# Top-k attention and a hard-swish feed-forward on one core: blocks of 128 tokens at an even rate, later reciprocals, and transposes of Keys and queries by DMA

## The chip, the cores and the metric

The kernel runs on one core of a Trainium2 chip. The core has five engines that work through their own queues of instructions in order and wait for each other by semaphores: TensorE (PE in the profile, with its weight loads as PEld) for matrix products, VectorE (DVE), ScalarE (ACT), GpSimd (POOL), and SyncE (SP), which here issues all DMAs. The metric is the device time of one execution in microseconds (us), lower is better; the median of several executions is compared.

## The reference

```python
q, k, v: (8, 8, 576, 64) float32            # batches, heads, tokens, head size
scores = (1 / sqrt(64)) * q @ k.T           # per batch and head: 576 x 576
kth = 32nd largest of each row
scores = where(scores >= kth, scores, -1e9)
attn = exp(scores - max); attn = attn / (sum(attn) + 1e-9)
x = (attn @ v) with the heads side by side  # 4608 tokens x 512
h = x @ w_in                                # 512 -> 2048
g = h * clip(h + 3, 0, 6) / 6
out = g @ w_out                             # 2048 -> 512
```

The two weight matrices arrive as float64 and are turned into float32 in the kernel.

## The kernel before, in words

**Units of work.** A *pair* is two heads of a batch (four pairs per batch, 32 in all). A *duo* is 128 queries of two pairs, which makes four rows of 576 scores on each partition, two per pair; the two pairs are the halves of the duo, u = 0 and 1. As 576 is 4 x 128 + 64, each batch has eight normal duos and two *rest* duos for the last 64 queries of both heads; a rest duo has half as many rows. Eight batches give 80 duos. In batches 0 to 2 the rest duos are at the end of the batch, in batches 3 to 6 they stand at places 2 and 7 of its ten duos (counted from 0), in batch 7 at places 2 and 3.

**One duo, in steps.** `scores` (L200 on): TensorE multiplies queries with Keys into the one large PSUM tile `big` (L215 to L230), ScalarE copies them to SBUF as `sc` (L219, L220, L233, L236; three buffers). `top` (L250, L254): VectorE finds the 32 largest of each row in four rounds of MAX8 and MATCH_REPLACE8. `shift` (L263, L266): GpSimd computes the bias of the exponential. `exp` (L273, L278, L283): ScalarE makes masked exponentials and their sums `den`. `inverse` (L287): VectorE takes the reciprocal of `den`. `weights` (L297, L306): GpSimd scales the rows and splits each float32 into two 16-bit halves, `e16`. `flip` (L312): SyncE issues a DMA transpose of those halves into `t16`. `join` (L318): ScalarE (u = 0) or GpSimd (u = 1) puts the halves together again as `eT`, now transposed. `values` (L338, L345): TensorE multiplies with the values into a PSUM tile `pv`, and ScalarE copies that at once to `xT` (for rest duos `xr`), the input of the feed-forward.

**Feed-forward.** A block is 128 or 256 tokens. The first product (L362) makes 512 columns of `h` at a time; ScalarE makes relu(h + 3) and a copy (L370, L372), GpSimd caps and multiplies (L376, L377); the second product (L384) sums up 16 parts for 128 tokens, ScalarE scales by 1/6 (L394) and SyncE stores. The generator `feed_forward` hands the work out in *pieces*: 16 for 128 tokens, 32 for 256. A piece of the first product is 16 TensorE instructions at 128 tokens and 8 of double width at 256; a piece of the second is 4. Each float32 product counts as two matmul instructions in the profile. The gates on GpSimd are issued two pieces behind their product.

**Order.** The order of all work is written out by hand: 80 x 8 slots and a few more at the end. In slot i of duo m VectorE's round i of the duo comes first, then the steps of this and earlier duos that are due by a table (`usual`, `early` for the first two duos, `soon` for the last two: the numbers are slots counted from the start of the duo), then some pieces. The scores of duo m + 1 are issued in slot 1 of duo m. How many pieces a duo gets is set at its start from `left`, the pieces that are queued: 6, 7, 8 or 9 for a normal duo, 3, 4, 4 or 5 for a rest duo, at less than 8, from 8, from 16 and from 48. A block takes 256 tokens where enough pieces are queued when its first half ends (L480, `state["half"]`). Ahead of value products, pieces are issued without a break until the buffer of `xT` that is to be written is free (`while ... piece()`).

**Keys and queries.** For each pair `load` (L146 on) brings Keys and queries to SBUF. `transpose` (L171 on) turns them on TensorE, nine transposes (L177) into `big`, and ScalarE copies to `kq` and `kr` (L179, L180, L183). The pairs of the next batch are loaded in slot 0 of duos 4 to 7 of a batch and transposed in slot 5 of duos 5 to 8.

Of the kernel before, what the change touches and what calls it, by code (L numbers as in the profile page):

```python
# [10 lines left out]
F32 = mybir.dt.float32  # L11
# [18 lines left out]
def kernel(  # L30
# [22 lines left out]
    def pool(name, bufs, **kw):  # L53
        return ctx.enter_context(tc.tile_pool(name=name, bufs=bufs, **kw))

    consts = pool("consts", 1)
    kqpool = pool("kq", 13)
    scpool = pool("sc", 3)
    wkpool = pool("wk", 1)
    mpool = pool("m", 4)  # L60
    xtpool = pool("xt", 2)
    xrpool = pool("xr", 1)
    gpool = pool("g", 8)
    hpool = pool("h", 2)
# [74 lines left out]
    class Pair:  # L139
# [31 lines left out]
        def transpose(self):  # L171
            kq = kqpool.tile([P, JP + S], F32, tag="kq", name="kq")
            self.kT, self.qT = kq[:, 0:JP], kq[:, JP : JP + S]
            ps = big()
            for j in range(2 * J + 1):
                rows = self.landed[:, j, :, :].rearrange("p h d -> p (h d)")
                nc.tensor.transpose(ps[:, j * P : (j + 1) * P], rows, ident[:])  # L177
            c0 = 2 * JP
            nc.scalar.copy(kq[:, 0:c0], ps[:, 0:c0])  # L179
            nc.scalar.copy(kq[:, c0 : c0 + R], ps[:, c0 + R : c0 + 2 * R])  # L180
            for hh in range(2):
                d = slice(hh * D, (hh + 1) * D)
                nc.scalar.copy(self.kr[d, hh, :], ps[d, c0 : c0 + R])  # L183

    class Duo:

# [139 lines left out]
        def values(self, dst):  # L326

            w = R if self.rest else P
            pv = ps_w.tile([P, 512], F32, tag="w", name="pv")
            for u in range(2):  # L330
                pr, eT = self.pairs[u], self.eT[u]
                for c in range(J + 1):
                    for hh in range(2):
                        if self.rest:
                            rhs = eT[:, c if c < J else J + hh, hh * R : (hh + 1) * R]
                        else:
                            rhs = eT[:, c if hh == 0 or c == J else J + 1 + c, :]
                        nc.tensor.matmul(  # L338
                            pv[hh * D : (hh + 1) * D, u * w : (u + 1) * w],
                            pr.vm[:, hh, c, :] if c < J else pr.vr[:, hh, :],  # L340
                            rhs,
                            start=(c == 0),
                            stop=(c == J),
                        )
            nc.scalar.copy(dst, pv[:, 0 : 2 * w].rearrange("p (u q) -> p u q", u=2))  # L345

    def feed_forward(xT, nt, rows):

        gs = []
        nf = 512 // nt
        for f0 in range(0, NFC, nf):
            h = ps_w.tile([P, 512], F32, tag="w", name="h")
            for f in range(f0, f0 + nf):
                if f == f0 + nf // 2:
                    yield None  # L360
                for i in range(NHP):
                    nc.tensor.matmul(  # L362
                        h[:, (f - f0) * nt : (f - f0 + 1) * nt],
                        w_in[:, i, f * P : (f + 1) * P],
                        xT[:, i, 0:nt],
                        start=(i == 0),
                        stop=(i == NHP - 1),
                    )
            g = gpool.tile([P, 512], F32, tag="g", name="g")
            nc.scalar.activation(g[:], h[:], AF.Relu, bias=three[:], scale=1.0)  # L370
            hs = hpool.tile([P, 512], F32, tag="h", name="hs")
            nc.scalar.copy(hs[:], h[:])  # L372
            gs.append(g)

            def gate(g=g, hs=hs):
                nc.gpsimd.tensor_scalar(g[:], g[:], 6.0, 0.0, ALU.min, ALU.max)  # L376
                nc.gpsimd.tensor_tensor(g[:], g[:], hs[:], ALU.mult)  # L377

            yield gate
        for t0 in range(0, nt, P):  # L380
            acc = ps_w.tile([P, DM], F32, tag="w", name="acc")
            for f in range(NFC):
                c0 = f % nf * nt + t0
                nc.tensor.matmul(  # L384
                    acc[:],
                    gs[f // nf][:, c0 : c0 + P],
                    w_out[:, f, :],
                    start=(f == 0),
                    stop=(f == NFC - 1),
                )  # L390
                if f % 2 == 1:
                    if f == NFC - 1:
                        o = opool.tile([P, DM], F32, tag="o", name="o")
                        nc.scalar.mul(o[:], acc[:], 1.0 / 6.0)  # L394
                        for p0, p1, dst in rows(t0):
                            nc.sync.dma_start(dst, o[p0:p1, :])
                    yield None

# [40 lines left out]
    def queue(*block):  # L441
        nonlocal left
        todo.append(feed_forward(*block))
        if block[0] is not state.get("xr"):
            blocks.append(todo[-1])
        left += block[1] // 8

    state = {}

    def values(m):  # L450

        u = duos[m]
        b, qt, hp = u.pairs[0].b, u.qt, u.pairs[0].hp
        if u.rest:
            if b % 2 == 0 and hp == 0:
                while state.get("rest") in todo:
                    piece()
                state["xr"] = xrpool.tile([P, NHP, P], F32, tag="xr", name="xr")
            u.values(state["xr"][:, hp : hp + 2, (b % 2) * R : (b % 2 + 1) * R])
            if b % 2 == 1 and hp == 2:  # L460

                def rows(t0):
                    return [
                        (i * R, (i + 1) * R, out[(b - 1 + i) * S + JP : (b + i) * S, :])
                        for i in range(2)
                    ]

                queue(state["xr"], P, rows)
                state["rest"] = todo[-1]
            return  # L470

        if hp == 0 and not state.get("half"):
            while len(blocks) > 1 and blocks[-2] in todo:
                piece()
            state["xT"] = xtpool.tile([P, NHP, 2 * P], F32, tag="xT", name="xT")
        c0 = P if state.get("half") else 0
        u.values(state["xT"][:, hp : hp + 2, c0 : c0 + P])
        if hp == 0:
            return
        state["half"] = not c0 and b < B - 1 and qt % 2 == 0 and left >= (24 if b < 3 else 4)  # L480
        if not state["half"]:

            def rows(t0):
                t = qt - c0 // P + t0 // P
                return [(0, P, out[b * S + t : b * S + JP : J, :])]

            queue(state["xT"], c0 + P, rows)

    chunks = list(weight_chunks())
    landing, converting, adding = [], [], []  # L490
# [25 lines left out]
    def pair_at(m, first):  # L516

        b, at = divmod(m, per_batch)
        return pairs[b + 1][at - first] if b + 1 < B and 0 <= at - first < NHP else None
# [16 lines left out]


    usual = dict(
        shift0=3, exp0=4, inverse0=7, weights0=8, flip0=10, join0=13,
        shift1=7, exp1=8, inverse1=11, weights1=12, flip1=14, join1=17, values=20,  # L540
    )
    early = dict(
        shift0=3, exp0=3, inverse0=4, weights0=4, flip0=5, join0=8,
        shift1=7, exp1=7, inverse1=8, weights1=8, flip1=9, join1=12, values=12,
    )
    soon = dict(
        shift0=3, exp0=3, inverse0=5, weights0=5, flip0=7, join0=10,
        shift1=7, exp1=7, inverse1=9, weights1=9, flip1=11, join1=14, values=16,
    )
    queued = {}  # L550
    for m in range(ND):
# [3 lines left out]
    def parts(slot, late=None):  # L555

        for m, part in sorted(queued.get(slot, []), key=lambda x: x[1][:-1] != "shift"):
            if late is not None and (part[:-1] in ("inverse", "weights")) != late:
                continue
            if part == "values":  # L560
                values(m)
            else:
                getattr(duos[m], part[:-1])(int(part[-1]))

    for m in range(ND + 3):
        u = duos[m] if m < ND else None

        level = (left >= 8) + (left >= 16) + (left >= 48)
        count = ((3, 4, 4, 5) if u and u.rest else (6, 7, 8, 9))[level]
        for i in range(8):  # L570
            if u:
                u.top(i // 4, i % 4)
# [14 lines left out]
                for p in duos[i // 4].pairs:  # L587
                    p.load_values()
            if i == 0:
                p = pair_at(m, 4)  # L590
                if p:
                    p.load()
            if i == 3 and u and u.pairs[0].b and 1 <= m % per_batch <= 2:
                for p in duos[m - 1].pairs:
                    p.load_values()
            if i == 5:
                p = pair_at(m, 5)
                if p:
                    p.transpose()
            piece((i + 1) * count // 8 - i * count // 8)  # L600
    while todo:
        piece()
    piece(2)
# [33 lines left out]
```

## Time and profile before

| | before |
|---|---|
| median of 10 executions | 1628.43 us (1627.47 to 1630.53) |
| the profiled execution | 1628.88 us |
| its span, first to last instruction | 1627.1 us |
| TensorE, VectorE busy | 1468.9 us, 1465.8 us |
| GpSimd, ScalarE busy | 1140.1 us, 1094.6 us |
| mean granted clock of TensorE | 0.960 |

In a row of the profile, L312 is line 312 of the kernel; `out<-in` are the program's names of the tiles; xN is a count; `busy, mean` are us in all and ns of one instruction; behind the second bar stands the idle time of the engine just before them, and what ended it. Rows of the chain and of the timeline begin with the start and the length in us; in brackets stands the idle time before and what ended it. Rows of waits read: who (engine, tile, line) waited for whom, us in total, times, longest.

### The profile page before, as it was taken

What the parts mean: (1) busy time and instruction counts of PE and PEld (TensorE: products, weight loads), DVE (VectorE), ACT (ScalarE), POOL (GpSimd) and SP (SyncE); (2) the same over time, 40 slices, a digit from 0 to 9 for tenths busy, and PEclk for the clock granted to TensorE, in tenths of its full rate; (3) what the DMA queues carried; (4) which work ended last, traced back from release to release, by engine and by line L of the source; (5) the groups of instructions that cost most, each with busy time, mean ns of one, the idle gap of its engine ahead of it and who ended that gap; (6) DMA issues with size and microseconds to landing.
All of it is one profiled execution on the core that took longest, in us unless ns stands there. A gap on an engine that the chain in (4) does not pass through costs nothing.

```text
span 1627.1 us, 26916 instructions
## 1 busy us (share of the span) xinstructions
PE 1468.9 (90%) x9376; PEld 999.9 (61%) x9376; DVE 1465.8 (90%) x3105; ACT 1094.6 (67%) x1865; POOL 1140.1 (70%) x1264
## 2 busy tenths in 40 slices
PE   5254989889999999988989999899999999899999
PEld 2152657566666776666657575647567584657875
DVE  6999999999999978999999999999999989999500
ACT  6675876767776577667768676767777676757521
POOL 4778676777867776766678596767687776867741
PEclk9577999999999999999999999999999999999999
DMA  8552543445334442445344533444454424433310
GB/s 229 149 181 59 95 99 71 84 98 95 73 87 90 87 88 52 102 88 109 71 86 87 114 66 80 99 101 83 75 101 93 94 56 92 83 62 71 65 22 13
DMA packets 450312, 144.37 MB, mean 89 GB/s; under 512 B 433280, under 2 KB 441472, under 8 KB 450176
## 3 DMA queue, kind: packets, MB, share of 16 engines
q1 hardware_dynamic: 450176, 142.65, 42.5%
q8 instruction: 74, 1.21, 0.3%
q14 instruction: 62, 0.51, 0.1%
HBM read 45.09 MB, written 9.44 MB: 34 GB/s over the span
## 4 chain that ended last, share of the span: by engine, by line
DVE 55%; PE 32%; POOL 7%; ACT 4%; issue 2%; SPq 1%; DMA 0%; POOLq 0%; ACTq 0%
DVE m L250 29%; DVE wk L254 24%; PE acc L384 12%; PE h L362 12%; PE pv L338 4%; PE big L227 2%; POOL e L306 1%; POOL eT L318 1%; POOL w_out L123 1%; POOL sc L297 1%; ACT sc L278 1%; ACT eT L318 1%; PE big L230 1%; ACT sc L273 1%; POOL a L109 1%
## 5 line engine op out<-in xcount | busy, mean ns | idle before, releaser
L250 DVE MAX8 m<-wk 128x8 f32<-128x576 f32 x864 | 615.5, 750 | 3.3
L384 PE MATMUL acc<-w_out,g 128*128 128x512 f32 x1152 | 521.8, 603 | 16.2 <-POOL g L377 16.2
L362 PE MATMUL h<-xT,w_in 128*128 128x128 f32 (+1 forms) x3200 | 476.1, 308 | 0.0
L362 PEld LDWEIGHTS h<-xT,w_in 128*128 128x128 f32 x3200 | 435.4, 194 | 33.4 <-issue 10.8
L254 DVE MATCH_REPLACE8 wk<-m,wk 128x576 f32<-128x576 f32 x576 | 424.4, 744 | 0.0
L384 PEld LDWEIGHTS acc<-w_out,g 128*128 128x128 f32 x1152 | 214.3, 193 | 256.4 <-issue 234.6
L306 POOL COPY e<-sc 128x2304 uint16<-128x2304 uint16 (+1 forms) x192 | 320.0, 1676 | 10.1
L338 PE MATMUL pv<-eT,vm 128*64 128x128 f32 (+1 forms) x2560 | 167.6, 276 | 102.1 <-POOL eT L318 55.6
L273 ACT ACTIVATE sc<-sc,m 128x576 f32<-128x576 f32 x288 | 209.7, 772 | 49.5 <-DVE m L250 49.1
L278 ACT ACTIVATE sc<-sc,shift 128x576 f32<-128x576 f32 x288 | 219.7, 765 | 16.8 <-POOL shift L266 13.7
L297 POOL TENSOR_SCALAR sc<-sc,den 128x576 f32<-128x576 f32 x288 | 214.6, 755 | 19.2 <-DVE den L287 18.6
L263 POOL TENSOR_TENSOR shift<-m 128x2 f32<-128x2 f32 (+1 forms) x160 | 33.2, 208 | 277.6 <-DVE den L287 275.3
L338 PEld LDWEIGHTS pv<-eT,vm 128*64 128x64 f32 x2560 | 136.0, 142 | 146.3 <-POOL eT L318 61.2
L318 ACT COPY eT<-t 128x2304 uint16<-128x2304 uint16 (+1 forms) x82 | 214.4, 2615 | 1.9 <-DMA t<-e 1.9
L254 DVE MATCH_REPLACE8 wk<-m,sc 128x576 f32<-128x576 f32 x288 | 212.1, 744 | 0.0
L318 POOL COPY eT<-t 128x2304 uint16<-128x2304 uint16 (+1 forms) x78 | 202.7, 2599 | 5.8 <-DMA t<-e 4.3
L250 DVE MAX8 m<-sc 128x8 f32<-128x576 f32 x288 | 203.3, 744 | 1.3 <-ACT sc L236 1.3
L377 POOL TENSOR_TENSOR g<-g,hs 128x512 f32<-128x512 f32 x144 | 184.2, 1279 | 12.1
L345 ACT COPY xT<-pv 128x256 f32<-128x256 f32 x64 | 23.8, 372 | 208.1 <-PE pv L338 208.1
L227 PE MATMUL big<-kq 64*128 64x512 f32 x512 | 134.9, 646 | 23.2 <-ACT kr L183 19.8
L376 POOL TENSOR_SCALAR g<-g 128x512 f32<-128x512 f32 x144 | 88.5, 614 | 88.2 <-ACT g L370 77.7
L370 ACT ACTIVATE g<-h,three 128x512 f32<-128x512 f32 x144 | 98.7, 686 | 66.1 <-PE h L362 63.4
(47 smaller groups left out, 1199.0 us busy)
## 6 DMA issues: line engine op xcount, KB each, us to landing
landed<-in_k_dram SPq DMA_DIRECT2D x64, 128.0 KB, 3.1
landed<-in_q_dram SPq DMA_DIRECT2D x64, 128.0 KB, 3.0
st<-in_moe_w_in_dram SPq DMA_DIRECT2D x16, 512.0 KB, 5.1
vm<-in_v_dram SPq DMA_DIRECT2D x64, 128.0 KB, 2.3
st<-in_moe_w_out_dram SPq DMA_DIRECT2D x16, 512.0 KB, 5.5
out_dram<-o SPq DMA_DIRECT2D x32, 256.0 KB, 2.4
t<-e SPq DMA_TRANSPOSE x160, 4.6
landed<-in_k_dram SPq DMA_DIRECT2D x32, 32.0 KB, 2.7
```

What stands on the lines that cost most here:

```text
L227: nc.tensor.matmul(banks[:, 2 * i + hh, :], pr.qT[d, qs], pr.kT[d, :])
L250: nc.vector.max(self.m[u][:, t, 8 * r : 8 * r + 8], self.cur[t])
L254: nc.vector.match_replace(wk, self.m[u][:, t, 8 * r : 8 * r + 8], self.cur[t], LOWEST)
L273: nc.scalar.activation(row, row, AF.Prelu, bias=m[:, t, TOP_K - 1 : TOP_K], scale=-1.0, alpha=FLAT)
L278: nc.scalar.activation(row, row, AF.Exp, bias=self.less[u][:, t : t + 1], scale=-scale / FLAT, accum_out=self.den[:, u, t : t + 1],)
L297: nc.gpsimd.tensor_scalar(row, row, self.den[:, u, t : t + 1], 1.0, ALU.mult, ALU.mult)
L306: nc.gpsimd.tensor_copy(halves[:, :, to : to + c1 - c0], words)
L318: copy(eT[:, 0 : self.nb, :] .rearrange("p c q -> p (c q)") .bitcast(U16) .rearrange("p (x h) -> p h x", h=2), self.t16[u][:, 0 : 2 * self ...
L338: nc.tensor.matmul(pv[hh * D : (hh + 1) * D, u * w : (u + 1) * w], pr.vm[:, hh, c, :] if c < J else pr.vr[:, hh, :], rhs, start=(c == 0), ...
L362: nc.tensor.matmul(h[:, (f - f0) * nt : (f - f0 + 1) * nt], w_in[:, i, f * P : (f + 1) * P], xT[:, i, 0:nt], start=(i == 0), stop=(i == NH ...
L377: nc.gpsimd.tensor_tensor(g[:], g[:], hs[:], ALU.mult)
L384: nc.tensor.matmul(acc[:], gs[f // nf][:, c0 : c0 + P], w_out[:, f, :], start=(f == 0), stop=(f == NFC - 1),)
```

## The change

- Every block of the feed-forward has 128 tokens; `xT` is half as large and has three buffers instead of two, and the loop ahead of value products now asks for the block three back instead of two.
- The pieces are issued at an even rate: one per slot while any is due, 1/8 more from 24 queued pieces on and again from 48 on, and half of that in rest duos.
- In the usual schedule the reciprocals, and all steps behind them, are two slots later. The first two duos and the last two keep their slots.
- The copy of `pv` is a step of its own, `place`, one slot behind `values`; the block is queued there.
- Keys and queries of all batches but the first are no longer turned on TensorE: GpSimd splits them into 16-bit halves, SyncE issues a DMA transpose, and ScalarE puts the halves together into `kq` and `kr`. The loads are one duo earlier; split is in slot 2 and flip in slot 5 of the duo behind the load, join in slot 1 of the one after. The pool that holds these tiles has 14 buffers instead of 13.

```diff
-    kqpool = pool("kq", 13)
+    kqpool = pool("kq", 14)
-    xtpool = pool("xt", 2)
+    xtpool = pool("xt", 3)
...
+        def split(self):
+
+            self.e16 = kqpool.tile([P, 2 * (2 * J + 1) * P], U16, tag="kq", name="e16")
+            nc.gpsimd.tensor_copy(
+                self.e16[:].rearrange("p (h x) -> p h x", h=2),
...
+        def flip(self):
+            self.t16 = kqpool.tile([P, 2 * (2 * J + 1), P], U16, tag="kq", name="t16")
+            nc.sync.dma_start_transpose(self.t16[:], self.e16[:])
+
+        def join(self):
+            kq = kqpool.tile([P, JP + S], F32, tag="kq", name="kq")
...
+            def copy(dst, src):
+                nc.scalar.copy(dst.bitcast(U16).rearrange("p (x h) -> p h x", h=2), src)
+
+            c0 = 2 * JP
+            copy(kq[:, 0:c0], halves[:, :, 0:c0])
+            copy(kq[:, c0 : c0 + R], halves[:, :, c0 + R : c0 + 2 * R])
+            for hh in range(2):
+                d = slice(hh * D, (hh + 1) * D)
+                copy(self.kr[d, hh, :], halves[d, :, c0 : c0 + R])
...
-            nc.scalar.copy(dst, pv[:, 0 : 2 * w].rearrange("p (u q) -> p u q", u=2))
+            self.pv = dst, pv[:, 0 : 2 * w].rearrange("p (u q) -> p u q", u=2)
+
+        def place(self):
+            nc.scalar.copy(*self.pv)
...
-            while len(blocks) > 1 and blocks[-2] in todo:
-                piece()
-            state["xT"] = xtpool.tile([P, NHP, 2 * P], F32, tag="xT", name="xT")
...
+                while len(blocks) > 2 and blocks[-3] in todo:
+                    piece()
+                state["xT"] = xtpool.tile([P, NHP, P], F32, tag="xT", name="xT")
...
     usual = dict(
-        shift0=3, exp0=4, inverse0=7, weights0=8, flip0=10, join0=13,
-        shift1=7, exp1=8, inverse1=11, weights1=12, flip1=14, join1=17, values=20,
+        shift0=3, exp0=4, inverse0=9, weights0=10, flip0=12, join0=15,
+        shift1=7, exp1=8, inverse1=13, weights1=14, flip1=16, join1=19, values=22, place=23,
     )
...
-        level = (left >= 8) + (left >= 16) + (left >= 48)
-        count = ((3, 4, 4, 5) if u and u.rest else (6, 7, 8, 9))[level]
...
-                p = pair_at(m, 4)
+                p = pair_at(m, 3)
...
-            if i == 5:
-                p = pair_at(m, 5)
+            for at, first_at, part in ((2, 4, "split"), (5, 4, "flip"), (1, 5, "join")):
+                p = pair_at(m, first_at) if i == at else None
                 if p:
-                    p.transpose()
-            piece((i + 1) * count // 8 - i * count // 8)
+                    getattr(p, part)()
+
+            due += ((left > 0) + (left >= 24) / 8 + (left >= 48) / 8) / (2 if u and u.rest else 1)
+            piece(int(due))
+            due -= int(due)
```

## The prediction

> **What bounds the kernel now.** I read the page first, for the busy shares, the slices and the chain.
>
> ```profile
> span 1627.1 us, 26916 instructions
> PE 1468.9 (90%) x9376; PEld 999.9 (61%) x9376; DVE 1465.8 (90%) x3105; ACT 1094.6 (67%) x1865; POOL 1140.1 (70%) x1264
> DVE  6999999999999978999999999999999989999500
> DVE 55%; PE 32%; POOL 7%; ACT 4%; issue 2%; SPq 1%; DMA 0%; POOLq 0%; ACTq 0%
> ```
>
> Two engines are equally full, and they are full at different times: VectorE (DVE) has no work in the last two and a half slices of 40.7 us, while TensorE (PE) works to the end. So there are two questions: what holds VectorE up before it ends, and how much of TensorE's work is left then. For the first I read the table of waits:
>
> ```profile
> DVE den L287 <- ACT den L283: 42.3, 19, 7.1
> DVE a L117 <- POOL a L109: 17.1, 6, 10.2
> ACT xT L345 <- PE pv L338: 208.1, 60, 8.2
> ```
>
> Nearly all of VectorE's idle time behind the start is the reciprocal (L287) that stands in its queue before ScalarE (ACT) has the row sums. The longest of these waits in the timeline:
>
> ```profile
> 609.63 1.20 PE L177 MATMUL big<-ident,landed 128*128 128x128 f32 x9
> 609.74 0.37 ACT L345 COPY xT<-pv 128x256 f32<-128x256 f32 x1 [3.53 <-PE pv L338]
> 611.78 0.20 ACT L283 ACTIVATE den<-den 128x1 f32<-128x1 f32 x1
> 612.02 0.16 DVE L287 RECIPROCAL den<-den 128x1 f32<-128x1 f32 x1 [7.14 <-ACT den L283]
> ```
>
> ScalarE stood 3.53 us for TensorE's weighted values, the exponentials queued behind that copy came late, and VectorE stood 7.14 us. TensorE was late, the two in-order engines passed it on. For the second question, VectorE's end (that of the last MAX8, 1527.59 + 1.41 = 1529.0) and the chain behind it:
>
> ```profile
> 1527.59 1.41 DVE L250 MAX8 m<-wk 128x8 f32<-128x576 f32 x2
> 1528.59 2.77 POOL L318 COPY eT<-t 128x2304 uint16<-128x2304 uint16 x1
> 1533.73 0.17 DVE L287 RECIPROCAL den<-den 128x2 f32<-128x2 f32 x1 [4.73 <-ACT den L283]
> ```
> ```profile
> 1475.93 1.92 PE big L227 x8
> 1478.49 3.57 PE h L362 x32
> ...
> 1519.43 2.33 PE pv L338 x40
> 1521.77 12.21 PE acc L384 x28
> 1533.98 14.29 PE h L362 x128
> 1548.28 13.73 PE acc L384 x32
> ...
> 1609.39 13.75 PE acc L384 x32
> ```
>
> A tail of 1627.1 - 1529.0 = 98.1 us is feed-forward on TensorE, without a gap. A piece (what one call of the work list issues) is 16 matmuls of the first product, 14.29 / 8 = 1.79 us, or 4 of the second, 13.73 / 8 = 1.72; say 1.75. Followed through the code, 35 pieces are due when VectorE's last slot ends and the last block brings 16: 51 x 1.75 + 2 x 2.33 for two value products = 93.9, and 1529.0 + 93.9 = 1622.9, against 1609.39 + 13.75 = 1623.1 in the chain. The last step, 4.0 us, is the scaling, the store and the end.
>
> **Why TensorE is late: a sum per batch.** VectorE's pace is that of the reciprocals, one per half of a duo:
>
> ```profile
> 231.14 0.15 DVE L287 RECIPROCAL den<-den 128x2 f32<-128x2 f32 x1
> 236.81 0.14 DVE L287 RECIPROCAL den<-den 128x1 f32<-128x1 f32 x1
> ...
> 299.67 0.15 DVE L287 RECIPROCAL den<-den 128x2 f32<-128x2 f32 x1
> 309.37 0.16 DVE L287 RECIPROCAL den<-den 128x2 f32<-128x2 f32 x1
> ```
>
> 9.70 us for half a normal duo (last two rows), 5.67 for half a rest duo (first two); a batch has eight and two: 8 x 19.4 + 2 x 11.34 = 177.9 us. TensorE in a batch: 72 pieces (4.5 blocks of 128 tokens by 16) x 1.75 = 126.0; ten times scores at 1478.49 - 1475.93 = 2.56, 25.6; ten value products at 2.33, 23.3; four pairs' transposes at 1.20, 4.8: 179.7 us. TensorE is asked for 1.8 us more than VectorE's time lasts.
>
> **The change, part by part.** *Transposes of Keys and queries off TensorE* (28 of 32 pairs): 28 x 1.20 = 33.6 us less, and a batch falls to 174.9, 3.0 under VectorE's. In their place stand, for each pair, a split on GpSimd (POOL), a DMA transpose on SyncE's queue and other copies on ScalarE.
>
> ```profile
> L306 POOL COPY e<-sc 128x2304 uint16<-128x2304 uint16 x128 | 269.1, 2102 | 8.1
> L318 ACT COPY eT<-t 128x2304 uint16<-128x2304 uint16 x66 | 183.7, 2784 | 1.9 <-DMA t<-e 1.9
> L179 ACT COPY kq<-big 128x1024 f32<-128x1024 f32 x32 | 32.1, 1005 | 6.9 <-PE big L177 6.8
> L180 ACT COPY kq<-big 128x64 f32<-128x64 f32 x32 | 7.1, 221 | 0.0
> L183 ACT COPY kr<-big 64x64 f32<-64x64 f32 x64 | 13.4, 209 | 0.4
> DMA to landing us min/median/max: 3.6/4.6/6.5
> ```
>
> The split has the shape of L306: 2.10 us, 58.9 in all, GpSimd to some 1199. ScalarE copies 2304 half-words a pair: by L318 2048/2304 x 2.78 = 2.47 for the large one, and three small ones at 0.2 to 0.4 (L180 and L183 below, their doubled length above): 3.1 to 3.7, taken 3.3, against 1.00 + 0.22 + 2 x 0.21 = 1.64 today: +46 us, to some 1141. Both lie beside VectorE: 1199 and 1141 of its 1490. That is nothing on the path as an average; without that cover a slot with split, weights and join on GpSimd delays the shift, and so the exponentials, by up to 2.1 us, and a pair's copies hold ScalarE 1.7 us longer, which I put into the residue below. The DMA transpose is of the size of the 160 there are; it lands in 3.6 to 6.5 us (last row), and the join stands four slots, about one half-duo of 9.7, behind its issue; flips, loads and stores behind it on SyncE's queue come one such issue later, with spare slots too.
>
> *All blocks of 128.* Seven blocks of 256 become fourteen.
>
> ```profile
> L362 PE MATMUL h<-xT,w_in 128*128 128x128 f32 x2304 | 272.1, 278 | 0.0
> L362 PE MATMUL h<-xT,w_in 128*128 128x256 f32 x896 | 204.0, 384 | 0.0
> L362 PEld LDWEIGHTS h<-xT,w_in 128*128 128x128 f32 x3200 | 435.4, 194 | 33.4 <-issue 10.8 <-PE pv L338 0.3
> ```
>
> A block of 128 takes 272.1 / 18 = 15.1 us of busy time, half of a 256 block 204.0 / 14 = 14.6: 14 x 0.5 = +7 us at most (the loads run beside the products), 2 a batch over the last batches, inside the 3.0 that are spare. I take 0 on the path. By the Trainium skill, "TensorE: Matmul & The Clock Gate", section "Back-to-back issue gap", a matmul costs about 81 ns at width 128 and 131 at 512 in a stream with loads, so narrow ones cost much more per column: a straight line gives an estimate of 98 at 256, and a factor 162/98 for these blocks, +133 us on 204. The two rows above, 118 ns against 228 per matmul, do not agree with it for f32, and the rows decide.
>
> *The even rate.* One piece per slot while any is due, half as many in rest duos: 8 x 8 + 2 x 4 = 72 per batch, what a batch brings, and no forced runs of pieces ahead of value products (before there are five, the last of 20 pieces behind VectorE's last slot). Followed through the code, 24 pieces are due when VectorE's slots end, and 16 come: 40 instead of 51.
>
> *Reciprocals two slots later, values copied a slot late.* The 42.3 us hold 4.73 behind VectorE's end and some 0.7 in the first duos, whose schedule stays: 36.9 can go. Two slots are about half of 9.70 (4.8 us) or of 5.67 (2.8); a mean wait is 42.3 / 19 = 2.2, and of the longest, 7.14, ScalarE's own wait for TensorE was 3.53, which the late copy and the lighter TensorE remove. I leave a residue of 3 us, for the load added to ScalarE and GpSimd; bounds 0 and, if half stays, 18. Behind the reciprocals the weights, flips, joins and value products of usual duos move by two slots; the score buffer (three) is then freed three slots, 7 us, before its next copy instead of five, and that copy has seven slots before VectorE needs it: 0. The last two duos keep their schedule, so the tail gets nothing from it. What is late next is VectorE's own work.
>
> **The sum.** VectorE ends at 1529.0 - 36.9 + 3 = 1495.1. Behind it TensorE waits for the last-but-one duo's join as now (1528.59 + 2.77 - 1529.0 = 2.4), then value product 2.3, 8 pieces 13.7, value product 2.3 (its operand: 4.7 to the reciprocal, about 3.7 scale and split, 4.6 flip, 2.8 join, 16 us behind VectorE's end, in time for 18.4), then two blocks at 14.3 + 13.7, 56.0, and 4.0: 80.7. Span 1575.8. The profiled execution took 1628.88, 1.8 over its span and 0.4 over the median of 1628.43: a median of **1577 us**.
>
> **The rivals.** *Stalls stay at the rest duos* (chance 0.12). Short slots there leave ScalarE and GpSimd the work of full duos; a pair's new work can fall on them. For it: the second rest duo of batches 3 to 6 (place 7 of ten) holds a split and a join, the first of batches 0 to 2 (place 8) a join. Against: the 2.8 us or more of new slack. Price: half of 36.9, 18 us: 1592.
> *The backlog does not shrink* (0.05): TensorE trails VectorE when it ends, so that the tail stays at 98: 1495 + 98 + 1.4 = 1594. Against: 174.9 under 177.9.
> *Narrow products cost their loads* (0.04), the case of slower. If the 896 added loads, 435.4 / 3200 = 0.136 us each, were not hidden, TensorE has 122 us more in the last four batches, where 3.0 x 4 = 12 are spare; 110 come out behind VectorE's end: 1687. It decides once more than about 60 us (half of the loads) are bare. Against: 128 such matmuls with their loads took 14.29 us, 0.112 each. This is where the skill's rule quoted above would lead.
> *The change does not take the waits away* (0.04): the late reciprocals wait as long, since ScalarE's lateness has another source; only the tail gains: 1577 + 34 = 1611.
>
> **How the numbers follow.** My forecast has 0.75. The range runs from 1566 (no residue, 3; no wait for the join, 2; some 6 of VectorE's small waits at L117 gone) to 1600, over the two mild rivals. A change of 0.2%, 3 us, is what a measurement of this kernel can tell. Faster: 0.75 + 0.12 + 0.05 + some of the last, 0.93; slower 0.05; within 0.2%, 0.02.
>
> **What would show it.** Right: wait of L287 below 8 us in all; VectorE's last MAX8 near 1495; ScalarE's wait for pv far under 208; TensorE's busy time near 1468.9 - 34 = 1435, GpSimd near 1199, ScalarE near 1141; a tail of about 81 us with two blocks behind the last value product. Wrong: new waits of VectorE for scores or row sums at the rest duos, ScalarE waiting for the new transposes, the first product above 15.1 us a block, or a TensorE clock (PEclk) lower than before's.

## The result, and the profile after

The changed kernel takes 1588.93 us (median of 8, 1587.86 to 1590.97) against 1628.65 (29 executions beside it): a ratio of 0.9758, 95% interval 0.9749 to 0.9766. The forecast was 1577, its range 1566 to 1600. The direction and most of the size came as forecast; 12 us of the 51 forecast are missing.

The head of the page after:

```profile
span 1588.3 us, 28285 instructions
PE 1448.8 (91%) x10020; PEld 1009.9 (64%) x10020; DVE 1467.2 (92%) x3105; ACT 1141.6 (72%) x1865; POOL 1197.5 (75%) x1292
DVE  6999999999999999999999999999999999899800
```

GpSimd and ScalarE have the load that was worked out (1199 and 1141). VectorE does the same work and ends earlier. Its waits, and ScalarE's wait for the weighted values:

```profile
DVE den L317 <- ACT den L313: 18.6, 8, 8.3
DVE m L280 <- ACT sc L266: 4.5, 3, 2.7
ACT xT L378 <- PE pv L368: 67.9, 34, 5.3
```

And VectorE's end in the timeline, with the last reciprocal behind it:

```profile
1500.53 1.41 DVE L280 MAX8 m<-wk 128x8 f32<-128x576 f32 x2
1510.27 0.17 DVE L317 RECIPROCAL den<-den 128x2 f32<-128x2 f32 x1 [8.34 <-ACT den L313]
```

Two terms can be read off. VectorE ends at 1500.53 + 1.41 = 1501.9, 27.1 us earlier than before (forecast: 33.9 earlier, 1495.1). The tail behind it is 1588.3 - 1501.9 = 86.4 instead of 98.1 (forecast 80.7). So 7 us are missing ahead of VectorE's end and 6 behind it. Of the 18.6 us of waits for the row sums, 8.3 lie behind the end; 10.3 remain where I had left 3.

The chain that ended last shows the tail:

```profile
1505.23 2.69 POOL eT L348
1507.96 2.40 PE pv L368 x20
1510.37 15.22 PE acc L415 x32
1525.59 2.33 PE pv L368 x40
1527.92 14.49 PE h L395 x128
1542.41 13.74 PE acc L415 x32
1556.14 14.29 PE h L395 x128
1570.43 13.75 PE acc L415 x32
```

The 40 pieces are there as counted: 32 matmuls of the second product ahead of the last value product, two whole blocks behind it. But the second half of the value product of duo 78 starts 1507.96 - 1501.94 = 6.0 us behind VectorE's end, and what follows runs slowly for a while. Why is in GpSimd's rows:

```profile
1494.75 2.76 POOL L348 COPY eT<-t 128x2304 uint16<-128x2304 uint16 x1 [1.92 <-DMA t<-e]
1497.60 0.61 POOL L409 TENSOR_SCALAR g<-g 128x512 f32<-128x512 f32 x1
1498.29 1.28 POOL L410 TENSOR_TENSOR g<-g,hs 128x512 f32<-128x512 f32 x1
1499.55 1.47 POOL L327 TENSOR_SCALAR sc<-sc,den 128x576 f32<-128x576 f32 x2
1501.09 2.10 POOL L336 COPY e<-sc 128x2304 uint16<-128x2304 uint16 x1
1503.28 0.61 POOL L409 TENSOR_SCALAR g<-g 128x512 f32<-128x512 f32 x1
1503.97 1.26 POOL L410 TENSOR_TENSOR g<-g,hs 128x512 f32<-128x512 f32 x1
1505.18 2.73 POOL L348 COPY eT<-t 128x2304 uint16<-128x2304 uint16 x1
1507.84 0.20 POOL L293 TENSOR_TENSOR shift<-m 128x2 f32<-128x2 f32 x1
```

The join of duo 77, now two slots later, waits 1.92 us for its DMA at the head of GpSimd's queue, and from there on the queue has no gap: gate, weights of duo 79, gate, the join of duo 78 (1505.18), and only then the shift of duo 79 (1507.84), for which ScalarE and VectorE's last reciprocal wait. Before, that join began at 1528.59, ahead of VectorE's end at 1529.0; now it begins 3.2 us behind it.

### The profile page after: what moved, and what is told of

It is laid out like the page before. It is cut to its first block, busy times and chain, and to the rows that moved or that the text cites. A ratio compares the mean times of both kernels' runs of the same rounds, so it can differ in the third digit from the quotient of the medians.

```text
span 1588.3 us, 28285 instructions
## 1 busy us (share of the span) xinstructions
PE 1448.8 (91%) x10020; PEld 1009.9 (64%) x10020; DVE 1467.2 (92%) x3105; ACT 1141.6 (72%) x1865; POOL 1197.5 (75%) x1292
## 4 chain that ended last, share of the span: by engine, by line
PE 56%; DVE 20%; POOL 13%; ACT 5%; issue 4%; DMA 1%; SPq 0%; POOLq 0%; ACTq 0%; DVEq 0%
PE acc L415 22%; PE h L395 19%; DVE m L280 10%; DVE wk L284 9%; PE pv L368 7%; PE big L257 5%; POOL eT L348 2%; POOL sc L327 2%; POOL e L336 2%; POOL g L410 2%; PE big L260 2%; ACT sc L308 1%; POOL a L109 1%; POOL e L188 1%; ACT eT L348 1%
## 5 line engine op out<-in xcount | busy, mean ns | idle before, releaser
L395 PE MATMUL h<-xT,w_in 128*128 128x128 f32 x4096 | 485.2, 279 | 2.5 <-ACT xT L378 2.5
L395 PEld LDWEIGHTS h<-xT,w_in 128*128 128x128 f32 x4096 | 473.7, 194 | 18.0 <-issue 12.9
L348 POOL COPY eT<-t 128x2304 uint16<-128x2304 uint16 (+1 forms) x78 | 203.3, 2606 | 12.6 <-DMA t<-e 12.5
L263 ACT COPY sc<-big 128x2048 f32<-128x2048 f32 (+1 forms) x65 | 119.5, 1838 | 38.5 <-PE big L260 38.0
L425 ACT ACTIVATE o<-acc 128x512 f32<-128x512 f32 x36 | 21.3, 592 | 103.3 <-PE acc L415 103.3
```

The lines of the kernel that those rows point to most:

```text
L348: copy(eT[:, 0 : self.nb, :] .rearrange("p c q -> p (c q)") .bitcast(U16) .rearrange("p (x h) -> p h x", h=2), self.t16[u][:, 0 : 2 * self ...
L395: nc.tensor.matmul(h[:, (f - f0) * P : (f - f0 + 1) * P], w_in[:, i, f * P : (f + 1) * P], xT[:, i, :], start=(i == 0), stop=(i == NHP - 1),)
```

## The experiments

The change has four parts: the late slots, the copy of the values in a step of its own, the even rate of pieces in blocks of 128, and the transposes by DMA. Each run below took one part alone, took one back, or changed one thing in the changed kernel. "VectorE ends" is the end of its last MAX8 in the profiled execution, "tail" the span behind it, "waits" VectorE's waits for row sums ahead of its end.

| kernel | median us | ratio to before (95%) | VectorE ends | tail | waits |
|---|---|---|---|---|---|
| before | 1628.43 | | 1529.0 | 98.1 | 37.6 |
| changed | 1588.93 | 0.9749 to 0.9766 | 1501.9 | 86.4 | 10.3 |
| e1 late slots alone | 1614.39 | 0.9899 to 0.9932 | 1509.5 | 102.4 | 22.5 |
| e2 DMA transposes alone | 1627.81 | 0.9986 to 1.0005 | 1526.0 | 98.4 | 36.4 |
| e3 even rate and blocks of 128 alone | 1604.70 | 0.9839 to 0.9869 | 1525.7 | 76.5 | 29.3 |
| e9 blocks of 128 alone | 1630.76 | 1.0009 to 1.0028 | 1546.0 | 82.9 | 56.1 |
| e4 changed, TensorE transposes | 1581.98 | 0.9701 to 0.9730 | 1495.0 | 85.3 | 5.5 |
| e11 as e4, with an unused split | 1590.34 | 0.9756 to 0.9785 | 1503.9 | 85.9 | 12.6 |
| e5 changed, old slots | 1589.77 | 0.9751 to 0.9784 | 1508.0 | 79.0 | 17.1 |
| e7 changed, values copied at once | 1587.95 | 0.9739 to 0.9768 | 1507.6 | 79.9 | 11.1 |
| e6 changed, old blocks and counts | 1619.83 | 0.9933 to 0.9962 | 1514.3 | 103.6 | 24.5 |
| e8 changed, last joins on ScalarE | 1583.32 | 0.9710 to 0.9739 | 1502.0 | 79.7 | 10.4 |
| e12 as e4, duos 76 and 77 in old slots | 1578.78 | 0.9687 to 0.9715 | 1494.3 | 83.1 | 5.3 |
| e13 as e4, last joins on ScalarE, more pieces | 1601.89 | 0.9825 to 0.9854 | 1532.3 | 68.6 | 43.9 |

e3 and e7 leave out a part of the result: the stores of a batch's normal blocks all go to the rows of its last such block, and the other rows are not written. The stores are as many and as large, and in each of the two kernels SyncE waits twice, 4.0 us in all, for a store before another.

### One part alone (e1, e2, e3)

```diff
 e1
-        shift0=3, exp0=4, inverse0=7, weights0=8, flip0=10, join0=13,
-        shift1=7, exp1=8, inverse1=11, weights1=12, flip1=14, join1=17, values=20,
+        shift0=3, exp0=4, inverse0=9, weights0=10, flip0=12, join0=15,
+        shift1=7, exp1=8, inverse1=13, weights1=14, flip1=16, join1=19, values=22,
```

> The kernel before, with the usual schedule's reciprocals and all behind them two slots later; blocks, piece counts, transposes and the copy of the values stay. Theory A (TensorE is asked for more than VectorE's time, and what VectorE stops losing appears as TensorE lateness): VectorE's waits for den fall from 42.3 to 5 to 15 us in all, but the tail behind its last MAX8 grows from 98 by 5 to 15 us; 1605 to 1620 us. Rival B (the slots are all there is to it): waits below 10 us, tail unchanged at 98, about 1594 us. Rival C (lateness has another source, the waits only move): 1625 us or more.

Measured 1614.39 us. VectorE's waits in e1:

```profile
DVE den L287 <- ACT den L283: 30.5, 7, 9.9
```

As theory A has it in total, not in its parts: 22.5 us of waits remain ahead of VectorE's end, more than the 5 to 15 expected, in fewer and longer pieces (7 in all instead of 19; the longest 9.9 us instead of 7.1). Two slots cover the short waits; the long ones stay. The tail grew by 4 us, less than the 5 to 15 expected.

```diff
 e2
+        (split, flip and join of the changed kernel)
-                p = pair_at(m, 4)
+                p = pair_at(m, 3)
-            if i == 5:
-                p = pair_at(m, 5)
+            for at, first_at, part in ((2, 4, "split"), (5, 4, "flip"), (1, 5, "join")):
+                p = pair_at(m, first_at) if i == at else None
                 if p:
-                    p.transpose()
+                    getattr(p, part)()
```

> The kernel before, with Keys and queries of batches 1 to 7 turned by split, DMA transpose and join, and nothing else changed (13 buffers in the pool, as before). Theory A: TensorE is relieved by some 34 us and comes back in time, so that VectorE's waits of 42.3 us fall to 15 to 30; the tail stays near 98 because its 51 pieces are set by the order of the program; 1605 to 1618 us. Rival C (the work added to GpSimd and ScalarE costs as much as TensorE gains): waits as before or longer, 1628 us or more.

Measured 1627.81 us: no change. TensorE's busy time fell, VectorE's waits did not. The head of e2's page and its waits:

```profile
PE 1449.6 (89%) x9124; PEld 977.7 (60%) x9124; DVE 1465.4 (90%) x3105; ACT 1146.3 (71%) x1865; POOL 1198.1 (74%) x1292
```
```profile
DVE den L317 <- ACT den L313: 41.1, 17, 8.6
```

19 us less on TensorE (1468.9 to 1449.6) bought nothing on balance. That is against theory A as I had put it, and nearest to rival C; e2 adds work on GpSimd and ScalarE too and cannot part the two. The places of the waits say more. In the kernel before, five runs of pieces are forced ahead of value products; four of them lie ahead of VectorE's end, in duos 26, 28, 67 and 76. The first reciprocal of each of these duos is late: duo 28's by 7.14 us (612.02, the longest wait, shown in the prediction), the others' by

```profile
573.24 0.17 DVE L287 RECIPROCAL den<-den 128x2 f32<-128x2 f32 x1 [5.25 <-ACT den L283]
1307.33 0.16 DVE L287 RECIPROCAL den<-den 128x1 f32<-128x1 f32 x1 [6.50 <-ACT den L283]
1470.35 0.17 DVE L287 RECIPROCAL den<-den 128x2 f32<-128x2 f32 x1 [2.65 <-ACT den L283]
```

These four are 21.5 of the 37.6 us. e2 has the same forced runs, and its waits at the same four reciprocals are 5.22, 5.58, 8.58 and 2.65 us, 22.0 in all: less work on TensorE, with more on GpSimd and ScalarE, did not shorten them.

```diff
 e3
-    xtpool = pool("xt", 2)
+    xtpool = pool("xt", 3)
...
-            piece((i + 1) * count // 8 - i * count // 8)
+            due += ((left > 0) + (left >= 24) / 8 + (left >= 48) / 8) / (2 if u and u.rest else 1)
+            piece(int(due))
+            due -= int(due)
```

> The kernel before, with blocks of 128 tokens, the even rate of pieces and three half-size buffers of xT; reciprocals, transposes and the copy of the values as before. Theory A: 40 pieces instead of 51 behind VectorE's end, tail about 81 to 85, and without forced runs the longest waits (7.1 and 6.5 us) go, the many short ones at rest duos stay: den waits 20 to 35 us; 1598 to 1612 us. Rival C (narrow products cost TensorE more than their half): first-product busy time up by 60 us or more and the tail longer than 98: above 1640 us.

Measured 1604.70 us, inside theory A's bounds: the tail is 76.5, even shorter than expected (followed through the code, 37 pieces stand behind the value products of duo 78, against 40 in the changed kernel), and the waits ahead of VectorE's end are 29.3. Nothing in it points to a cost of narrow products.

### The DMA transposes taken back (e4), and what of them costs (e11)

e4 is the changed kernel with `load` and `transpose` where they were before.

> The changed kernel with Keys and queries turned on TensorE as before (loads a duo later, as before). Theory A: TensorE has 34 us more to do with some 21 spare, so it trails VectorE at its end by 5 to 15 us, and the rest duos wait a little longer: 1595 to 1610 us. Rival B (the DMA way buys nothing; its work on GpSimd and ScalarE is what causes the 10 us of waits that are left): 1580 to 1590 us, the waits for den in the middle below 9 us.

Measured 1581.98 us: the changed kernel is *slower* than this one, by 7 us, as rival B has it. VectorE in e4 ends where I had forecast it for the change:

```profile
1493.62 1.41 DVE L280 MAX8 m<-wk 128x8 f32<-128x576 f32 x2
```

1495.0. TensorE is full in e4 and yet hardly delays VectorE: in the table by stretches (PE, PEld, DVE, ACT and POOL busy, then clock, DMA share and GB/s) it is busy all the time, and VectorE nearly so.

```profile
800.00:1000.00 200.00, 200.00 (x1428) 140.15 (x1427) 199.14 (x428) 144.80 (x250) 150.00 (x166) 1.00 0.48 92
```

Which part of the DMA way costs the 7 us? e11 keeps TensorE's transposes and makes the split on GpSimd too, for nothing:

```diff
 e11, against e4
-                p = pair_at(m, 4)
+                p = pair_at(m, 3)
+            if i == 2:
+                p = pair_at(m, 4)
+                if p:
+                    p.split()
```

> The changed kernel with TensorE's transposes, and with the split on GpSimd made in the changed kernel's place all the same, its result unused. Theory S (the 2.1 us of GpSimd per pair are what the DMA way costs): 1586 to 1590 us, VectorE ends near 1501. Rival J (ScalarE's longer copies, or the transposes by DMA, are what costs): 1581 to 1584 us, VectorE ends near 1495.

Measured 1590.34 us: theory S, just over its bound. VectorE ends at 1503.9, 8.9 later than in e4. The rows of the split and of VectorE's waits in e11:

```profile
L188 POOL COPY e<-landed 128x2304 uint16<-128x2304 uint16 x28 | 59.0, 2107 | 0.0
```
```profile
DVE den L317 <- ACT den L313: 23.1, 12, 10.5
```

59 us of GpSimd work, 2.1 us at a time, cost VectorE 9 us although GpSimd is idle a quarter of the time. e11 also loads a pair one duo earlier, as the changed kernel does; that was not tried apart from the split. The changed kernel differs from e11 by the longer copies on ScalarE and the DMA transposes, and by 22 us less on TensorE (1448.8 against 1471.2); it is no slower. Those three together cost nothing that these runs can tell; they were not parted.

### The late slots and the late copy taken back (e5, e7)

```diff
 e5
-        shift0=3, exp0=4, inverse0=9, weights0=10, flip0=12, join0=15,
-        shift1=7, exp1=8, inverse1=13, weights1=14, flip1=16, join1=19, values=22, place=23,
+        shift0=3, exp0=4, inverse0=7, weights0=8, flip0=10, join0=13,
+        shift1=7, exp1=8, inverse1=11, weights1=12, flip1=14, join1=17, values=20, place=21,
```

> The changed kernel with the usual schedule's reciprocals and all behind them back in their old slots (the copy of the values still one slot behind its products). Theory A (lateness of TensorE is the source, the slots only cover it): waits for den 10 to 18 us more in the middle, the tail shorter by up to 9 us, since the last usual duos no longer meet the last two on GpSimd; 1588 to 1597 us. Theory D, formed after the first four runs (the reciprocals' slots alone decide VectorE's waits, the old slots bring nearly all 37 us back): VectorE ends at 1520 to 1530, 1597 to 1610 us.

Measured 1589.77 us, the time that theory A expected, and against theory D; the waits ahead of VectorE's end differ by 6.8 us (17.1 against 10.3), less than the 10 to 18 expected. The late slots bring VectorE's end forward by 6.1 us (1508.0 to 1501.9) and give 7.4 back in the tail (79.0 to 86.4): inside this change they are worth nothing on balance. 3.5 of the 7.4 are pieces: in e5 38 of them stand behind the value products of duo 78, in the changed kernel 40.

```diff
 e7
-            self.pv = dst, pv[:, 0 : 2 * w].rearrange("p (u q) -> p u q", u=2)
+            nc.scalar.copy(dst, pv[:, 0 : 2 * w].rearrange("p (u q) -> p u q", u=2))
...
-        ... values=22, place=23,
+        ... values=22,
```

> The changed kernel with the weighted values copied in the slot of their products again, and the block queued there. Theory A' (the late copy takes ScalarE's waits for the products, which the late reciprocals would cover anyway): ScalarE's waits for pv rise from 83 to 110 to 140 us, 1587 to 1592 us. Rival (ScalarE's waits reach VectorE): VectorE ends 5 us or more later, 1594 us or more.

Measured 1587.95 us: the late copy is worth nothing on balance either. ScalarE's waits for pv are 131.7 instead of 83.1, as theory A' has it. VectorE ends 5.7 us later, which looks like the rival, but its waits for row sums ahead of the end are 11.1 against 10.3; what grew are its waits for the weights' conversion at the start (`a`, L117: 20.2 against 13.7 us, all before 150 us). The tail is 6.5 shorter, with the late slots in place and 39 pieces behind the value products of duo 78.

### The pieces (e6, e9)

e6 is the changed kernel with blocks of 128 and 256, two full buffers of `xT` and the piece counts of before, with 13 buffers in the pool of Keys and queries.

> The changed kernel with the blocks, buffers of xT and piece counts of before (13 buffers in the pool of Keys and queries, for room). Theory A' (order alone sets the tail, 51 pieces instead of 40; forced runs ahead of value products bring some long waits of the reciprocals back): VectorE ends at 1503 to 1510, tail 98 to 105, 1603 to 1616 us. Rival (the even rate only moves pieces, TensorE makes up for it): 1589 to 1595 us.

Measured 1619.83 us, 31 more than the changed kernel and 4 over the expected range: the tail is 103.6, as expected, VectorE ends at 1514.3, 4 later than expected, and its waits are back at 24.5 us. With the late slots, the late copy and the DMA transposes all in place, only 8 us of the 40 are left. The even rate, with the blocks and buffers that it needs, carries most of the change.

```diff
 e9, against before
-        state["half"] = not c0 and b < B - 1 and qt % 2 == 0 and left >= (24 if b < 3 else 4)
+        state["half"] = not c0 and b < B - 1 and qt % 2 == 0 and False
```

> The kernel before, with all blocks of 128 tokens and nothing else changed (its piece counts then leave 41 pieces behind VectorE's slots instead of 51, with more forced runs on the way). Theory A': first product's busy time up by 7 to 10 us, tail 80 to 88, waits for den 36 to 45 us; 1610 to 1622 us. Rival (narrow products cost their loads): first product up by 60 us or more, above 1640 us.

Measured 1630.76 us: both expectations missed. The tail (82.9) is as expected, but VectorE's waits rose:

```profile
DVE den L287 <- ACT den L283: 62.9, 22, 7.8
```
```profile
L362 PE MATMUL h<-xT,w_in 128*128 128x128 f32 x4096 | 486.2, 279 | 0.0
```

The products themselves cost 486.2 + 59.4 (for `xr`) against 272.1 + 204.0 + 59.8 before: 9.7 us more. What was lost is 56.1 - 37.6 = 18.5 us of waits. Followed through the code, e9 issues seven runs of 3 to 10 pieces ahead of value products instead of five, four of them in batches 4 and 6: in duos 45, 47, 65 and 67. The longest waits are the first reciprocals of three of these, 7.40 us in duo 47 and, in duos 65 and 67,

```profile
1287.02 0.17 DVE L287 RECIPROCAL den<-den 128x2 f32<-128x2 f32 x1 [7.83 <-ACT den L283]
1326.06 0.16 DVE L287 RECIPROCAL den<-den 128x1 f32<-128x1 f32 x1 [7.41 <-ACT den L283]
```

In the kernel before, duos 47 and 65 have no such run and no such wait. Blocks of 128 are no gain in themselves; they allow the even rate, which needs no such runs.

### The tail, and a last attempt (e8, e12, e13)

```diff
 e8
-    for u in duos[:2]:
+    for u in duos[:2] + duos[-2:]:
         u.early = True
```

> The changed kernel with the second joins of the last two duos on ScalarE instead of GpSimd. Theory T (GpSimd's queue at the end delays the join of duo 78 and the shift of duo 79): TensorE's idle 4 us and the slow clock behind it go, tail 79 to 82, 1582 to 1586 us. Rival U: 1588 to 1590 us.

Measured 1583.32 us, theory T. VectorE ends as in the changed kernel, the pieces behind it are the same 40, and the tail is 79.7. The chain of e8 has the second product behind the value product of duo 78 at full pace:

```profile
1502.72 2.33 PE pv L368 x40
1505.06 13.93 PE acc L415 x32
```

```diff
 e12, against e4
+    middle = dict(
+        shift0=3, exp0=4, inverse0=7, weights0=8, flip0=10, join0=13,
+        shift1=7, exp1=8, inverse1=11, weights1=12, flip1=14, join1=17, values=20, place=21,
+    )
...
-        for part, at in (early if m < 2 else soon if m >= ND - 2 else usual).items():
+        for part, at in (early if m < 2 else soon if m >= ND - 2 else middle if m >= ND - 4 else usual).items():
```

> The changed kernel with TensorE's transposes, and with the last two usual duos (76 and 77) in the old slots, all others as in the change. Theory T (the tail of 85 us holds some 9 us because the last usual duos' later joins and gates stand on GpSimd in front of the last two duos' steps): tail 76 to 79, 1572 to 1576 us. Rival U (the tail is longer for TensorE's own lateness): 1581 to 1584 us.

Measured 1578.78 us, the fastest of all, but between the two expectations: the tail is 83.1, 2.2 less than in e4 and not 9, and some 1.75 of the 2.2 is one piece less (39 behind the value products of duo 78). GpSimd still holds the join of duo 78 behind the weights of duo 79. That the tail's lengthening comes from the last usual duos is not shown; that GpSimd's queue holds 6 to 7 us of it is (e8).

e13 joins e4 and e8 and hurries the pieces, so that 34 instead of 40 are left:

```diff
 e13, against e4
-    for u in duos[:2]:
+    for u in duos[:2] + duos[-2:]:
...
-            due += ((left > 0) + (left >= 24) / 8 + (left >= 48) / 8) / (2 if u and u.rest else 1)
+            due += ((left > 0) + (left >= 12) / 8 + (left >= 48) / 8) / (2 if u and u.rest else 1)
```

> The changed kernel with TensorE's transposes, the last two duos' second joins on ScalarE, and the extra eighth of a piece from 12 queued pieces on instead of 24 (34 pieces then stand behind VectorE's slots instead of 40). If the two causes are as found: VectorE ends at 1495 to 1498, tail 68 to 72, 1564 to 1572 us. Rival (TensorE has no room before the end for six more pieces): 1574 to 1578 us, as without the last edit.

Measured 1601.89 us, 20 slower than e4, outside both expectations. The tail is 68.6 as expected. VectorE ends at 1532.3, 37 us later:

```profile
DVE den L317 <- ACT den L313: 47.2, 14, 6.5
```

One extra piece of 1.75 us per eight slots, in duos that have 12 to 23 pieces queued, is enough to bring VectorE's waits to 43.9 us, more than in the kernel before. e4 and e13 do the same work in nearly the same order. e4 and e8 joined without the last edit were not run, but the edit of e8 first acts at the join of duo 78, and the second reciprocal of duo 77, ahead of that, already stands at 1501.44 in e13 against 1471.11 in e4: 30 us are lost by then, to the pieces alone. How a piece more reaches ScalarE was not taken apart further.

## Why the prediction was right or wrong

**Right.** The two questions were the right ones: VectorE's waits for the row sums, and the pieces left behind its end. 40 pieces instead of 51 are in the trace, and the tail follows their number where GpSimd's queue does not hold it up (e8). ScalarE's wait for pv fell from 208 to 67.9, and GpSimd's and ScalarE's busy times came within 2 us. The narrow products cost as little as taken: 485.2 us / 4096 = 118 ns of busy time each, as before; the rule of the Trainium skill ("TensorE: Matmul & The Clock Gate", "Back-to-back issue gap") by which a narrow stream costs much more per column does not hold for these f32 products, in the changed kernel or in e9 (486.2 / 4096 = 119).

**Wrong: "nothing on the path as an average" for the work added to GpSimd, and with it the residue of 3 us.** I had compared GpSimd's total with VectorE's time. The split, with the load one duo earlier, costs 9 us of VectorE's time (e11 against e4), and the waits that remain are 10.3 us, with 3.4 us of waits for scores beside them. It was inside the bounds (0 to 18). The way that the sentence named, a split in front of a shift, is not what the trace shows: the five waits between the first duo and VectorE's end (1.00, 0.75, 1.47, 3.15 and 2.98 us) all stand, by the order of the program, in duos 19, 29, 42, 62 and 73, and none of these holds a split. How the split's 2.1 us get there stays open. Of the signs that the prediction gave, the waits for row sums below 8 us in all (18.6) and VectorE's last MAX8 near 1495 (1500.5) failed with this term.

**Wrong: the sum per batch as the cause.** TensorE was said to be asked for 1.8 us per batch more than VectorE's time, and the DMA transposes to be what turns that. The sum itself does not hold: it takes all ten duos at a normal duo's price, 2.56 us of scores and 2.33 of value products. In the profile before, the scores of a rest duo run from 205.67 to 207.76 and its value products from 261.96 to 263.27, where the next products start. Their first and last rows:

```profile
205.67 1.07 PE L215 MATMUL big<-kq 64*64 64x512 f32 x4
207.55 0.28 PE L217 MATMUL big<-kr,kq 64*64 64x64 f32 x4
261.96 0.69 PE L338 MATMUL pv<-eT,vm 128*64 128x64 f32 x16
263.06 0.29 PE L338 MATMUL pv<-eT,vr 128*64 128x64 f32 x4
```

That is 2.09 and 1.31 us, 3.0 less for the two rest duos of a batch: 176.7 against VectorE's 177.9, and the excess is gone. Taking the transposes off TensorE alone changes nothing (e2), and putting them back makes the changed kernel 7 us faster (e4), with TensorE busy without a gap in the stretch quoted. Even TensorE's busy time fell by half of what was summed: 1465.7 us in e4 against 1448.8, 17 us and not 34. The rows of the transposes (L177) fall by 33.1 us, but those of the value products of normal duos grow by 7.1 (194.8 to 201.9), and rows overlap; the rest was not broken down. TensorE was late where the order asked for several pieces at once, as the waits behind the forced runs show, not because there was too much in total. A sum that comes out 1% over its limit cannot carry such a claim.

**Wrong: "the last two duos keep their schedule, so the tail gets nothing from it".** They keep their slots, but GpSimd's queue is full in front of them. The term that failed is the wait for the last-but-one duo's join, put at 2.4 us "as now": it was 6.0, and the slow clock behind it added over 2. That is the missing 6 of the forecast of 80.7, and e8 (79.7), which takes these joins off GpSimd, shows that it is GpSimd's queue. What the late slots have to do with it is less clear: of e5's 7.4 us, 3.5 are two pieces, and e7 has the late slots and a tail of 79.9, with TensorE back at work 3.6 us behind VectorE's end.

**The parts' worth.** Alone: even rate -23.7 us, late slots -14.0, DMA transposes -0.6. Taken from the change: even rate 31, late slots and late copy 1 or less each, DMA transposes -7. That the time fell inside the range is in part luck: the part that was to cure TensorE's lateness costs 7 us, and the even rate, whose gain was summed in the tail alone, also takes away the forced runs and the waits behind them.

**The rivals.** The stalls at the rest duos (1592) came nearest in time, and the trace bears out their place: duos 19, 29, 42, 62 and 73, where 9.4 of the 10.3 us of waits stand, are all rest duos. Their price was half of the 18 us given. That the split makes a part of the stalls is what e11 shows. That the backlog would not shrink, that narrow products would cost their loads and that the waits would stay are all refuted by the rows above. e13 shows what a rival should have been: TensorE's order, a little faster, costs VectorE more than the tail gains.

## What to carry to other kernels

In a kernel whose engines are all nearly three quarters full or more, a spare total on an engine is no cover: ask which instruction stands in front of which in its queue at the tightest place, and price a block of 2 us by the wait that it causes there. Take a many-part change apart before keeping all of it; here one part carried most of the gain, two were worth nothing on balance, and one cost 7 us. Here an order that spreads TensorE's work evenly was worth more than less work on TensorE, and what it leaves for the end can be counted in the code.

## What the runs showed of the hardware

TensorE's clock fell by half after a wait of 4.1 us at the end of the changed kernel. The row of the wait, and the table by stretches with the granted clock behind the busy times:

```profile
1507.96 1.97 PE L368 MATMUL pv<-eT,vm 128*64 128x128 f32 x16 [4.08 <-POOL eT L348]
```
```profile
1503.50:1507.90 4.40, 0.39 (x8) 0.14 (x4) 0.00 (x0) 0.00 (x0) 4.32 (x4) 0.80 0.71 134
1507.90:1512.00 4.10, 4.04 (x22) 2.84 (x23) 0.17 (x1) 3.59 (x9) 3.69 (x7) 0.50 0.00 0
```

The clock is 0.50 in the 4.1 us behind the wait: 16 matmuls take 1.97 us instead of 1.09 (their pace in e8), and the 32 of the second product 15.22 instead of 13.74. A wait of 4.1 us so costs over 2 us more. The Trainium skill ("TensorE: Matmul & The Clock Gate", "What's actually happening") says that an idle window of about 3.4 us brings half the rate, and as much of work the full one; after this wait the trace agrees. In e8, where the longest wait there was 2.13 us, the same 32 matmuls took 13.93.

The length of one wait does not decide it alone. In e4 the wait at this place was 2.45 us, and the clock fell all the same; the 32 matmuls took 15.59:

```profile
1501.00:1505.00 4.00, 4.00 (x24) 2.28 (x25) 0.17 (x1) 3.56 (x9) 3.59 (x6) 0.65 0.00 0
```

Behind the wait of 2.14 us at 1497.56 in the changed kernel the clock stayed at 1.00 for the next 4.1 us.
